# A fused attention, expert and gated layer on one core: the last half block is stored behind the final branch

## The chip, the core and the metric

The kernel runs on one core of one Trainium2 chip. The core has TensorE (PE in the rows; PEld are its weight loads), VectorE (DVE), ScalarE (ACT), GpSimd (POOL), and SyncE (SP), which here issues most of the DMA transfers. A letter q behind an engine's name stands for its sequencer, which handles branches, semaphores and DMA issues. The metric is the time of one execution on the device in microseconds. Three runs of the kernel before took 420.01, 418.44 and 418.93 us, so the median is 418.93.

## The reference

Three layers follow each other, all in float32. A linear attention with 4 batches, 8 heads, 576 tokens and 64 columns per head compresses keys and values into 32 memory slots, and each query attends to these. Then every token goes through one of 8 experts, with a sticky choice: a gate decides whether the expert of the token before is kept. The last layer is a gated convolution over tokens.

```python
# experts
e = fresh_e if s == 0 or local_gate[b, s] < 0.5 else prev_e
h = np.maximum(x[b, s] @ w1[e], 0.0)
out[b, s] = p[e] * (h @ w2[e])
# gated layer
h = np.maximum(x @ w_in, 0.0)
for k in range(3):
    conv_out += conv_w[k][None, None, :] * hp[:, k:k + S, :]
return (h * (1.0 / (1.0 + np.exp(-conv_out))) @ w_out).astype(np.float32)
```

## The kernel before, in words

The kernel computes with the expert that the first token of each batch chooses, and finds out on the way whether any token chose another one. Their number is kept in `anyi`, a single integer. With the given inputs it is zero. The work up to 211 us (attention, expert products, routing) is ordered by hand in a list of items and is not touched by the change.

The function `gated` is the last layer. For each batch it multiplies by `w_in` (tiles `pi`), makes the gate on ScalarE, VectorE and GpSimd, and multiplies by `w_out` (tiles `po`), 128 tokens by 512 columns at a time. Each product is the sum of three products of high and low parts over eight blocks of 128, so 24 matmuls. The result goes from PSUM to `ot` by ScalarE (line 1052) and from there to `out` by SyncE (line 1054). A batch has four full chunks of 128 tokens; its last 64 tokens are collected by GpSimd in `tail` and are done for two batches together, as chunk 4. In the last batch the last chunk is done in two halves of 256 columns (lines 1043 to 1049), each evicted by ScalarE and stored by SyncE as soon as its 24 matmuls are through.

Behind that stands the branch (lines 1063 and 1064). Each engine loads `anyi` into a register, compares it with zero, and runs or jumps over the part that adds the other experts and repeats the gated layer. The skipped part lies between the branch and the end of the program, and each engine has its own branch in its own list of instructions. Where an engine jumps, it lands in a short block that waits until the engine's own work is done and adds to the engine's semaphore what the skipped part would have added, so that later waits read the same count on both ways. SyncE does this for each of its DMA queues. From there it is one step to the end block (line 1116 in the rows): SyncE waits in twelve instructions for all queues and engines, each engine runs a DRAIN, and two barriers led by GpSimd with a clearing of semaphores between them close the program.

A tile scheduler orders the instructions in each block, here in the order in which they are written, and sets the waits on semaphores. It moves nothing across a branch.

Of the kernel before, what the change touches and what calls it, by code (L numbers as in the profile page):

```python
# [114 lines left out]
def fused_kernel(tc, q, first, first_q, kv, kv_tail, phi, w1, w2, w_in, conv_w, w_out, out):  # L115
    nc = tc.nc
    wide = w_in.dtype == I64
    PSUM = bass.MemoryType.PSUM
    with (
# [2 lines left out]
        tc.tile_pool(name="state", bufs=2) as state,  # L122
        tc.tile_pool(name="wpool", bufs=4) as wpool,
        tc.tile_pool(name="ps1", bufs=4, space=PSUM) as ps1,
        tc.tile_pool(name="ps2", bufs=2, space=PSUM) as ps2,
    ):

        def bank(name):
            return ps1.tile([128, 512], F32, tag="one", name=name)

        def banks(name):
            return ps2.tile([128, 2, 512], F32, tag="two", name=name)

        def slow(item):

# [831 lines left out]
        def gated(gp, nm, scaled=False):  # L967
            def first(b):
                return None if scaled else expert(b)

            wo.clear()
            for j in range(4):
                stage_out(j)
            ys = y_parts(0) if scaled else ys0[1]
            if scaled:
                split_y(0, load_y(0, None), *ys)
            tail = None
            for b in range(B):
                yh, yl = ys
                gs = []  # L980
                if b + 1 < B:
                    yn = load_y(b + 1, first(b + 1))
                if b % 2 == 0:
                    tail = gp.tile([128, 8, 2, 128], F32R, tag="tail", bufs=1, name=f"tail{b}")
                to = 64 * (b % 2)
                def gate(f, ht, ct):
                    nc.scalar.activation(ct, ct, AF.Sigmoid)  # L987
                    slow(f"gm.{f}").tensor_tensor(ct, ht, ct, ALU.mult)  # L988
                    t = gp.tile([128, 2, S], F32R, tag="g", name=f"g{nm}{b}_{f}")

                    def finish():
                        split(t[:, 0, :], t[:, 1, :], ct, slow(f"gs.{f}"))
                        nc.gpsimd.tensor_copy(tail[:, f, :, to:to + 64], t[:, :, 512:576].bitcast(F32))  # L993

                    gs.append(t)
                    return finish

                before = None
                for f in range(8):
                    fs = slice(f * 128, (f + 1) * 128)  # L1000
                    ps = banks(f"pi{b}_{f}")
                    matmul3([(ps[:, hf, :HALF], half(hf)) for hf in range(2)],
                            [((wi[kc][:, 0, fs], wi[kc][:, 1, fs]), (yh[:, kc, :], yl[:, kc, :])) for kc in range(4)],
                            tc.keep_in_program_order if b == 0 else lambda ins: ins)
                    finish = gate(*before) if before else lambda: None
                    ht = lp.tile([128, S], F32, tag="cv", name=f"ht{b}_{f}")
                    nc.scalar.activation(two(ht), halves(ps), AF.Relu)  # L1007
                    ct = lp.tile([128, S], F32, tag="cv", name=f"ct{b}_{f}")
                    nc.scalar.activation(ct, ht, AF.Copy, scale=convw[:, 1, f:f + 1])  # L1009
                    nc.vector.scalar_tensor_tensor(  # L1010
                        ct[:, 1:], ht[:, :S - 1], convw[:, 0, f:f + 1], ct[:, 1:], ALU.mult, ALU.add)
                    nc.vector.scalar_tensor_tensor(  # L1012
                        ct[:, :S - 1], ht[:, 1:], convw[:, 2, f:f + 1], ct[:, :S - 1], ALU.mult, ALU.add)
                    finish()
                    before = f, ht, ct
                    while len(wo) < 4 and f >= WO[len(wo)]:
                        wo.append(w2_piece(f"wo{len(wo)}", slow(f"wo.{len(wo)}")))
                gate(*before)()
                if b + 1 < B:
                    ys = y_parts(b + 1)  # L1020
                    split_y(b + 1, yn, *ys)

                def product(ps, c, fr, cols=slice(0, 512)):
                    for f in fr:
                        w = wo[f // 2].rearrange("p s (i d) -> p s i d", i=2)
                        st = [gs[f][:, s, c * 128:(c + 1) * 128] if c < 4 else tail[:, f, s, :] for s in range(2)]
                        for i, (sp, mp) in enumerate(((0, 0), (0, 1), (1, 0))):
                            nc.tensor.matmul(ps[:, cols], st[sp], w[:, mp, f % 2, cols],  # L1028
                                             start=f == 0 and i == 0, stop=f == 7 and i == 2)

                chunks = [0, 1, 2] + [4] * (b % 2) + [3]
                pss = {c: bank(f"po{b}_{c}") for c in chunks[:3]}
                for c in chunks[:3]:
                    product(pss[c], c, range(0, 6))
                for c in chunks:
                    if c in pss:
                        product(pss[c], c, range(6, 8))
                    elif b < B - 1 or c != chunks[-1]:
                        pss[c] = bank(f"po{b}_{c}")
                        product(pss[c], c, range(8))  # L1040
                    else:

                        for cq in range(2):
                            cols = slice(256 * cq, 256 * cq + 256)
                            ps = bank(f"po{b}_{c}_{cq}")
                            product(ps, c, range(8), cols)
                            ot = gp.tile([128, 256], F32, tag="ot", bufs=4, name=f"ot{b}_{c}_{cq}")
                            nc.scalar.activation(ot, ps[:, cols], AF.Copy)
                            nc.sync.dma_start(out[b, c * 128:(c + 1) * 128, cols], ot)
                        continue  # L1050
                    ot = gp.tile([128, 512], F32, tag="ot", bufs=4, name=f"ot{b}_{c}")
                    nc.scalar.activation(ot, pss[c], AF.Copy)  # L1052
                    if c < 4:
                        nc.sync.dma_start(out[b, c * 128:(c + 1) * 128, :], ot)
                    else:
                        nc.sync.dma_start(out[b - 1, 512:576, :], ot[0:64])
                        nc.sync.dma_start(out[b, 512:576, :], ot[64:128])

        wo = []
        ffn_cm.__exit__(None, None, None)  # L1060
        with tc.tile_pool(name="gated", bufs=8, reuse_waits="tile") as gp:
            gated(gp, "")
        any_more = nc.values_load(anyi[0:1, 0:1], min_val=0, max_val=B * E)
        with tc.If(any_more > 0, preferred_fallthrough_block=True):
            with tc.tile_pool(name="more", bufs=1) as fp:
                fps.append(fp)
                for b in range(B):
                    other_experts(b)
            with tc.tile_pool(name="again", bufs=8, reuse_waits="tile") as gp:
                gated(gp, "x", True)  # L1070
        late[0].__exit__(None, None, None)


# [46 lines left out]
```

## Time and profile before

| what | value |
|---|---|
| median of three runs | 418.93 us |
| profiled execution | 418.69 us, its span 416.9 us |
| TensorE busy | 406.9 us, 98% of the span |
| VectorE, ScalarE, GpSimd busy | 276.2, 222.2 and 74.8 us |
| matmuls of line 1028 (`po`) | 90.2 us, 408 of them |
| granted TensorE clock, mean | 0.999 of full speed |

The span goes from the program's first to its last instruction; the time of the execution has some 1.8 us more around it. Branches, semaphores and DMA issues do not count as busy, so the end of the program, where nothing else runs, shows as idle in the busy shares; it can be read in the views of single lines, where those instructions stand with their durations and starts.

### The profile page before, as it was taken

The page shows a single profiled execution, that of the slowest core. Times are in us where ns is not written, and L with a number is a line of the kernel's source. Part 1 is how long each engine was busy: PE and PEld are TensorE (multiplying, and loading weights), DVE is VectorE, ACT ScalarE, POOL GpSimd, SP SyncE. Part 2 cuts the span into 40 slices and gives each one's busy share as a digit, 9 for nine tenths or more (in the row PEclk, how much of TensorE's full clock was granted, in tenths as well). Part 3 has the DMA queues.
Part 4 walks back from the last instruction along what each step waited for, and adds up shares of the span by engine and source line. Part 5 has one row for each costly group of instructions (what it writes and reads, how often), then busy time and mean ns, then how long its engine had stood idle before and what let it go on. Part 6 is the DMA issues. An engine that isn't in the chain of part 4 may idle for free.

```text
span 416.9 us, 8479 instructions
## 1 busy us (share of the span) xinstructions
PE 406.9 (98%) x3390; PEld 370.8 (89%) x3391; DVE 276.2 (66%) x509; ACT 222.2 (53%) x414; POOL 74.8 (18%) x121
## 2 busy tenths in 40 slices
PE   7999999999999999999999999999999999999994
PEld 6769989889989998899999988998889988999884
DVE  2679899696786984975979981579105792177500
ACT  4356568465566354745748652577215773277320
POOL 1000201411122211311111620033200332014300
PEclk9999999999999999999999999999999999999999
DMA  7999979976984599946550032000020000200022
GB/s 270 346 374 405 347 258 347 412 274 231 338 285 153 146 380 400 363 164 197 167 176 2 2 113 100 2 2 0 31 75 21 2 1 13 89 2 0 3 77 57
DMA packets 23760, 69.04 MB, mean 166 GB/s; under 512 B 3264, under 2 KB 4032, under 8 KB 23712
## 3 DMA queue, kind: packets, MB, share of 16 engines
q1 hardware_dynamic: 20128, 56.88, 38.6%
q0 software_dynamic: 3584, 11.54, 7.1%
q8 instruction: 28, 0.46, 0.4%
q14 instruction: 20, 0.16, 0.1%
HBM read 52.08 MB, written 16.33 MB: 164 GB/s over the span
## 4 chain that ended last, share of the span: by engine, by line
PE 91%; DMA 4%; SPq 1%; DVE 1%; ACT 1%; issue 0%; ACTq 0%
PE py L160 25%; PE pi L160 24%; PE po L1028 24%; PE ph L160 11%; DMA wb_0r<-in_w 2%; DMA kt<-in_kv_tail 2%; PE pk L406 1%; PE pv L449 1%; PE sc L449 1%; PE idle L456 1%; PE pa L384 1%; PE pl L587 1%; DVE wb L148 0%; SPq L271 0%; ACT wb L147 0%
## 5 line engine op out<-in xcount | busy, mean ns | idle before, releaser
L160 PE MATMUL py<-h,wb 128*128 128x288 f32 x768 | 108.2, 297 | 0.0
L160 PEld LDWEIGHTS py<-h,wb 128*128 128x128 f32 x768 | 102.9, 188 | 4.2 <-issue 3.2
L160 PE MATMUL pi<-yh,wi 128*128 128x288 f32 x512 | 90.4, 295 | 0.0
L1028 PE MATMUL po<-wo,g 128*128 128x512 f32 (+1 forms) x408 | 90.2, 377 | 0.0
L1028 PEld LDWEIGHTS po<-wo,g 128*128 128x128 f32 x408 | 72.8, 188 | 13.2
L160 PEld LDWEIGHTS pi<-yh,wi 128*128 128x128 f32 x512 | 76.3, 188 | 0.9
L1010 DVE SCALAR_TENSOR_TENSOR ct<-ht,convw,ct 128x575 f32<-128x575 f32 x32 | 30.9, 966 | 52.4 <-ACT ct L1009 52.4
L160 PE MATMUL pi<-yl,wi 128*128 128x288 f32 x256 | 54.6, 295 | 0.0
L160 PE MATMUL ph<-att,vh 128*128 128x288 f32 x256 | 53.5, 302 | 0.7 <-DVE h L753 0.3
L993 POOL CAST tail<-g 128x128 fp32r<-128x128 f32 x32 | 23.1, 724 | 122.9 <-DVE g L148 122.2
L160 PEld LDWEIGHTS ph<-att,vh 128*128 128x128 f32 x256 | 40.5, 188 | 4.9 <-DVE h L753 2.1
L836 POOL DMA_DIRECT2D ydram<-ys x32 | 17.5, 547 | 146.8 <-ACT ys L835 140.4
L160 PEld LDWEIGHTS pi<-yl,wi 128*128 128x128 f32 x256 | 41.1, 188 | 0.0
L1007 ACT ACTIVATE ht<-pi 128x576 f32<-128x576 f32 x32 | 20.8, 651 | 33.8 <-PE pi L160 33.8
L160 PE MATMUL ph<-att,vl 128*128 128x288 f32 x128 | 37.7, 296 | 0.0
L753 DVE SCALAR_TENSOR_TENSOR h<-ph,h 128x288 fp32r<-128x288 f32 x64 | 28.1, 450 | 13.3 <-ACT h L752 13.3
L752 ACT ACTIVATE h<-ph 128x288 fp32r<-128x288 f32 x64 | 25.7, 410 | 15.0 <-PE ph L160 14.7
L835 ACT ACTIVATE ys<-py 128x288 f32<-128x288 f32 x32 | 13.1, 409 | 37.1 <-PE py L160 24.5
L1052 ACT ACTIVATE ot<-po 128x512 f32<-128x512 f32 x17 | 9.5, 598 | 43.4 <-PE po L1028 43.4
L988 DVE TENSOR_TENSOR ct<-ht,ct 128x576 f32<-128x576 f32 x32 | 27.0, 844 | 7.3 <-ACT ct L987 7.1
L1012 DVE SCALAR_TENSOR_TENSOR ct<-ht,convw,ct 128x575 f32<-128x575 f32 x32 | 28.4, 886 | 0.4
L147 ACT ACTIVATE g<-ct 128x576 fp32r<-128x576 f32 x32 | 21.7, 680 | 12.6 <-DVE ct L988 12.6
(234 smaller groups left out, 505.1 us busy)
## 6 DMA issues: line engine op xcount, KB each, us to landing
kv<-in_kv SPq DMA_DIRECT2D x16, 512.0 KB, 8.6
q<-in_q SPq DMA_DIRECT2D x8, 576.0 KB, 9.5
ydram<-ys POOLq DMA_DIRECT2D x32, 144.0 KB, 5.2
y<-ydram SPq DMA_DIRECT2D x4, 1152.0 KB, 6.8
out<-ot SPq DMA_DIRECT2D x15, 256.0 KB, 2.1
ph<-in_phi SPq DMA_DIRECT2D x8, 288.0 KB, 7.3
adram<-at POOLq DMA_DIRECT2D x8, 288.0 KB, 7.0
wa_0r<-in_w SPq DMA_DIRECT2D x4, 512.0 KB, 4.0
```

The lines of the kernel that those rows point to most:

```text
L147: pin(nc.scalar.activation(hi, src, AF.Copy))
L160: pin(nc.tensor.matmul(ps, st, mv[:, cols], start=i == 0, stop=i == len(terms) - 1))
L752: nc.scalar.activation(t[:, 0, :], ps, AF.Relu)
L753: low = nc.vector.scalar_tensor_tensor(t[:, 1, :], ps, 0.0, t[:, 0, :].bitcast(F32), ALU.max, ALU.subtract)
L835: nc.scalar.activation(yt, ps, AF.Copy)
L836: stored.append(nc.gpsimd.dma_start(ydram[b, d, :, half(hf)], yt).ins)
L988: slow(f"gm.{f}").tensor_tensor(ct, ht, ct, ALU.mult)
L993: nc.gpsimd.tensor_copy(tail[:, f, :, to:to + 64], t[:, :, 512:576].bitcast(F32))
L1007: nc.scalar.activation(two(ht), halves(ps), AF.Relu)
L1010: nc.vector.scalar_tensor_tensor(ct[:, 1:], ht[:, :S - 1], convw[:, 0, f:f + 1], ct[:, 1:], ALU.mult, ALU.add)
L1012: nc.vector.scalar_tensor_tensor(ct[:, :S - 1], ht[:, 1:], convw[:, 2, f:f + 1], ct[:, :S - 1], ALU.mult, ALU.add)
L1028: nc.tensor.matmul(ps[:, cols], st[sp], w[:, mp, f % 2, cols], start=f == 0 and i == 0, stop=f == 7 and i == 2)
```

## The change

The last chunk's first half is copied out of PSUM by VectorE and stored by GpSimd, in place of ScalarE and SyncE. The second half goes into a PSUM tile `last` of its own, for which the pool of pairs `ps2` is closed and a pool `ps3` is opened in its place. Its eviction by ScalarE and its store by SyncE are written behind the branch and so stand in a block that follows both ways. A hint for TensorE's branch is placed behind the last matmul of chunk 4. Within the part that is skipped, `gated` does the same with its own last chunk.

```diff
--- before.py
+++ after.py
@@ -122,14 +122,18 @@
         tc.tile_pool(name="state", bufs=2) as state,
         tc.tile_pool(name="wpool", bufs=4) as wpool,
         tc.tile_pool(name="ps1", bufs=4, space=PSUM) as ps1,
-        tc.tile_pool(name="ps2", bufs=2, space=PSUM) as ps2,
     ):
+        ps2_cm = tc.tile_pool(name="ps2", bufs=2, space=PSUM)
+        pairs = [ps2_cm.__enter__()]
 
         def bank(name):
             return ps1.tile([128, 512], F32, tag="one", name=name)
 
         def banks(name):
-            return ps2.tile([128, 2, 512], F32, tag="two", name=name)
+            return pairs[-1].tile([128, 2, 512], F32, tag="two", name=name)
+
+
+        last_block = []
 
         def slow(item):
 
@@ -1025,8 +1029,8 @@
                         w = wo[f // 2].rearrange("p s (i d) -> p s i d", i=2)
                         st = [gs[f][:, s, c * 128:(c + 1) * 128] if c < 4 else tail[:, f, s, :] for s in range(2)]
                         for i, (sp, mp) in enumerate(((0, 0), (0, 1), (1, 0))):
-                            nc.tensor.matmul(ps[:, cols], st[sp], w[:, mp, f % 2, cols],
-                                             start=f == 0 and i == 0, stop=f == 7 and i == 2)
+                            last_product[:] = [nc.tensor.matmul(ps[:, cols], st[sp], w[:, mp, f % 2, cols],
+                                                                start=f == 0 and i == 0, stop=f == 7 and i == 2).ins]
 
                 chunks = [0, 1, 2] + [4] * (b % 2) + [3]
                 pss = {c: bank(f"po{b}_{c}") for c in chunks[:3]}
@@ -1040,13 +1044,21 @@
                         product(pss[c], c, range(8))
                     else:
 
-                        for cq in range(2):
-                            cols = slice(256 * cq, 256 * cq + 256)
-                            ps = bank(f"po{b}_{c}_{cq}")
-                            product(ps, c, range(8), cols)
-                            ot = gp.tile([128, 256], F32, tag="ot", bufs=4, name=f"ot{b}_{c}_{cq}")
-                            nc.scalar.activation(ot, ps[:, cols], AF.Copy)
-                            nc.sync.dma_start(out[b, c * 128:(c + 1) * 128, cols], ot)
+                        if not scaled:
+                            ps2_cm.__exit__(None, None, None)
+                            last_cm.append(tc.tile_pool(name="ps3", bufs=1, space=PSUM))
+                            pairs.append(last_cm[0].__enter__())
+
+                            with tc.issue_after(last_product[0]):
+                                tc.mark_branch_hint_location("more", engines=[ENG.PE])
+                            last_block.append(pairs[-1].tile([128, 512], F32, tag="last", name="last"))
+                        cols = slice(0, 256)
+                        ps = bank(f"po{b}_{c}")
+                        product(ps, c, range(8), cols)
+                        ot = gp.tile([128, 256], F32, tag="ot", bufs=4, name=f"ot{b}_{c}")
+                        nc.vector.tensor_copy(ot, ps[:, cols])
+                        nc.gpsimd.dma_start(out[b, c * 128:(c + 1) * 128, cols], ot)
+                        product(last_block[0], c, range(8), slice(256, 512))
                         continue
                     ot = gp.tile([128, 512], F32, tag="ot", bufs=4, name=f"ot{b}_{c}")
                     nc.scalar.activation(ot, pss[c], AF.Copy)
@@ -1056,18 +1068,22 @@
                         nc.sync.dma_start(out[b - 1, 512:576, :], ot[0:64])
                         nc.sync.dma_start(out[b, 512:576, :], ot[64:128])
 
-        wo = []
+        wo, last_cm, last_product = [], [], []
         ffn_cm.__exit__(None, None, None)
         with tc.tile_pool(name="gated", bufs=8, reuse_waits="tile") as gp:
             gated(gp, "")
         any_more = nc.values_load(anyi[0:1, 0:1], min_val=0, max_val=B * E)
-        with tc.If(any_more > 0, preferred_fallthrough_block=True):
+        with tc.If(any_more > 0, preferred_fallthrough_block=True, label="more"):
             with tc.tile_pool(name="more", bufs=1) as fp:
                 fps.append(fp)
                 for b in range(B):
                     other_experts(b)
             with tc.tile_pool(name="again", bufs=8, reuse_waits="tile") as gp:
                 gated(gp, "x", True)
+        ot = late[1].tile([128, 256], F32, tag="last", bufs=1, name="ot")
+        nc.scalar.activation(ot, last_block[0][:, 256:], AF.Copy)
+        nc.sync.dma_start(out[B - 1, 384:512, 256:], ot)
+        last_cm[0].__exit__(None, None, None)
         late[0].__exit__(None, None, None)
```

On TensorE, the place is the step from chunk 4 (tile `po_4`, from `tail`) to the last chunk's first half (`po_3_0`, now `po_3`; `wo` and `g` are the weights and the gated values). Before:

```order
L1028 MATMUL po_4_4821<-wo_3347,tail_4018 128x512 x6
L1028 MATMUL po_4_4821<-wo_3387,tail_4018 128x512 x6
L1028 MATMUL po_3_0_4850<-wo_3230,g_0_4499 128x256 x3
L1028 MATMUL po_3_0_4850<-wo_3230,g_1_4536 128x256 x3
L1028 MATMUL po_3_0_4850<-wo_3307,g_2_4573 128x256 x3
```

Now:

```order
L1032 MATMUL po_4_4821<-wo_3347,tail_4018 128x512 x6
L1032 MATMUL po_4_4821<-wo_3387,tail_4018 128x512 x6
L1132 BRANCH_PREFETCH_HINT
L1032 MATMUL po_3_4856<-wo_3230,g_0_4499 128x256 x3
L1032 MATMUL po_3_4856<-wo_3230,g_1_4536 128x256 x3
```

The hint is new between the two; the matmuls keep their order and their shapes, and behind them stand the load of `anyi` and the branch, as before.

On ScalarE, the place is the end of its list ahead of the branch (`ot_0` to `ot_2` and `ot_4` are full evictions, `anyi` is the flag). Before:

```order
L1052 ACTIVATE ot_2_4818<-po_2_4739 128x512
L1052 ACTIVATE ot_4_4846<-po_4_4821 128x512
L1048 ACTIVATE ot_3_0_4875<-po_3_0_4850 128x256
L1048 ACTIVATE ot_3_1_4903<-po_3_1_4878 128x256
L1063 TENSOR_LOAD anyi
L1064 COMPARE_AND_BRANCH
```

Now:

```order
L1064 ACTIVATE ot_1_4809<-po_1_4738 128x512
L1064 ACTIVATE ot_2_4818<-po_2_4739 128x512
L1064 ACTIVATE ot_4_4846<-po_4_4821 128x512
L1075 TENSOR_LOAD anyi
L1076 COMPARE_AND_BRANCH
```

The evictions of the two halves are gone from it. The second one stands in the new block, behind the jumps at the end of both ways:

```order
L1064 ACTIVATE ot_2_8795<-po_2_8716 128x512
L1064 ACTIVATE ot_4_8823<-po_4_8798 128x512
L1076 UNCONDITIONAL_BRANCH x2
L1084 ACTIVATE ot<-last 128x256
L1132 UNCONDITIONAL_BRANCH
```

It waits there for TensorE's semaphore with the count of the skipped part in it. SyncE's last store stands in the same block, behind SyncE's own jump.

On GpSimd, the place is the end of its work ahead of the branch (`tail` collects the last tokens). Before:

```order
L148 TENSOR_TENSOR g_6_4721<-ct_6_4687,g_6_4721 128x576
L993 CAST tail_4018<-g_6_4721 128x2x64
L993 CAST tail_4018<-g_7_4733 128x2x64
L1063 TENSOR_LOAD anyi
L1064 COMPARE_AND_BRANCH
```

Now:

```order
L152 TENSOR_TENSOR g_6_4721<-ct_6_4687,g_6_4721 128x576
L997 CAST tail_4018<-g_6_4721 128x2x64
L997 CAST tail_4018<-g_7_4733 128x2x64
L1060 DMA out<-ot_3_4881 128x256
L1075 TENSOR_LOAD anyi
L1076 COMPARE_AND_BRANCH
```

A store now stands between GpSimd's last copy and its load of the flag, and it waits for VectorE's copy of the first half. Behind the branch, on the way that is taken, GpSimd's list before is this (the first row holds the jumps of both ways; the row ahead of it belongs to the skipped part):

```order
L148 TENSOR_TENSOR gx_6_8696<-ct_6_8662,gx_6_8696 128x576
L993 CAST tail_7997<-gx_6_8696 128x2x64
L993 CAST tail_7997<-gx_7_8708 128x2x64
L1064 UNCONDITIONAL_BRANCH x2
L1116 ISA
```

And now this:

```order
L1060 DMA out<-ot_3_8852 128x256
L1076 UNCONDITIONAL_BRANCH
L1076 ISA
L1076 UNCONDITIONAL_BRANCH
L1132 UNCONDITIONAL_BRANCH
L1132 ISA
```

The instruction between the jumps adds the skipped part's store to its DMA semaphore, and one jump more leads through the new block.

## Rows read from the trace of the kernel before

**Rows 1.** Stretches: us; busy PE, PEld, DVE, ACT, POOL; clock, DMA, GB/s.
```profile
405.28:411.20 5.92, 5.91 (x49) 5.70 (x47) 0.00 (x0) 0.99 (x2) 0.00 (x0) 1.00 0.28 69
411.20:416.90 5.70, 0.00 (x0) 0.00 (x0) 0.00 (x0) 0.38 (x1) 0.00 (x0) 0.94 0.10 32
```

**Rows 2.** Timeline, the end: start us, us, engine, line, what, idle before.
```profile
408.40 0.39 ACT L1048 ACTIVATE ot<-po 128x256 f32<-128x256 f32 x1 [2.32 <-PE po L1028]
410.31 0.88 PE L1028 MATMUL po<-wo,g 128*128 128x256 f32 x6
411.28 0.38 ACT L1048 ACTIVATE ot<-po 128x256 f32<-128x256 f32 x1 [2.49 <-PE po L1028]
```

**Rows 3.** Line 1049, the last stores: min/median/max ns, starts; landing us.
```profile
L1049 SPq DMA_DIRECT2D out<-ot x2: 338/338/338, 408.8 to 411.7; - x2
DMA to landing us min/median/max: 1.7/1.7/1.7
```

**Rows 4.** Line 1064, the branch: ns, first and last start, by engine.
```profile
L1064 SPq EVENT_SEMAPHORE  x9: 17/17/17, 414.6 to 415.2; - x9
L1064 PEldq EVENT_SEMAPHORE  x2: 51/51/51, 413.1 to 413.3; - x2
L1064 ACTq EVENT_SEMAPHORE  x2: 17/17/17, 414.5 to 414.6; - x2
L1064 PEldq COMPARE_BRANCH  x1: 3602/3602/3602, 409.5 to 409.5; - x1
L1064 ACTq COMPARE_BRANCH  x1: 50/50/50, 411.8 to 411.8; - x1
L1064 SPq COMPARE_BRANCH  x1: 53/53/53, 412.1 to 412.1; - x1
L1064 POOLq EVENT_SEMAPHORE  x2: 17/17/17, 396.3 to 396.4; - x2
L1064 POOLq COMPARE_BRANCH  x1: 45/45/45, 393.5 to 393.5; - x1
```

**Rows 5.** DMA queues from 409 to 416 us: packets, MB, share.
```profile
q8 instruction: 2, 0.03, 2.1%
```

**Rows 6.** Line 1116, the end block, in several stretches, as rows 4.
```profile
L1116 SPq EVENT_SEMAPHORE  x12: 28/28/28, 415.3 to 416.0; - x12
L1116 POOLq DRAIN  x1: 4966/4966/4966, 396.5 to 396.5; - x1
L1116 ACTq DRAIN  x1: 8/8/8, 414.7 to 414.7; - x1
L1116 POOLq EVENT_SEMAPHORE  x4: 17/17/17, 416.2 to 416.8; - x4
L1116 POOLq DRAIN  x2: 44/76/107, 416.3 to 416.7; - x2
```

**Rows 7.** Timeline and line 1057: last eviction and store before the halves.
```profile
405.48 0.60 ACT L1052 ACTIVATE ot<-po 128x512 f32<-128x512 f32 x1 [4.84 <-PE po L1028]
L1057 SPq DMA_DIRECT2D out<-ot x1: 588/588/588, 406.6 to 406.6; - x1
```

**Rows 8.** Line 1063, GpSimd's load of the flag.
```profile
L1063 POOLq TENSOR_LOAD <-anyi x1: 486/486/486, 392.9 to 392.9; - x1
```

**Rows 9.** Groups by form, VectorE, 128x256: busy us, mean ns, idle.
```profile
L740 DVE TENSOR_TENSOR vl<-pv,vh 128x256 fp32r<-128x256 f32 x2 | 0.8, 419 | 0.1
```

**Rows 10.** Timeline and line 836: a GpSimd store behind ScalarE; landings, 180-190.
```profile
188.63 0.41 ACT L835 ACTIVATE ys<-py 128x288 f32<-128x288 f32 x1 [3.10 <-PE py L160]
189.34 0.54 POOL L836 DMA_DIRECT2D ydram<-ys  x1 [2.93 <-ACT ys L835]
DMA to landing us min/median/max: 2.4/2.9/3.7
```

**Rows 11.** Line 1107, the start block, GpSimd's DRAIN there.
```profile
L1107 POOLq DRAIN  x1: 184/184/184, 0.3 to 0.3; - x1
```

**Rows 12.** Timeline of GpSimd, its last work before the branch.
```profile
392.96 0.30 POOL L993 CAST tail<-g 128x128 fp32r<-128x128 f32 x1 [1.42 <-DVE g L148]
```

## The prediction

> **What bounds the kernel now.** I first cut the span into stretches of busy time [rows 1]. TensorE works 5.91 of the 5.92 us from 405.28, the two last half products, and not at all in the 5.70 behind them, where ScalarE works 0.38 us and nothing else does. The granted clock is 1.00 until the products end. The change touches nothing before 405.28 us: up to there each engine's list of instructions is the same in both programs. So the question is what the 5.70 us behind the last product are made of.
>
> The timeline comes next [rows 2]. The first half product lets ScalarE go at 408.40, the last product ends at 410.31 + 0.88 = 411.19, ScalarE evicts its 256 columns in 0.38 us from 411.28, and the store is issued at 411.7 and lands 1.7 us behind that [rows 3], near 413.4. That is still 3.5 us before the end.
>
> The rows of the branch say what fills them [rows 4]. Every engine reads a flag, compares and jumps over the part for other experts, because the flag is zero here. The jump is dear: SyncE compares at 412.1 and runs its next instruction, the first of nine semaphore rows, at 414.6; ScalarE goes 411.8 to 414.5; TensorE's compare alone lasts 3602 ns, 409.5 to 413.1; GpSimd went 393.5 to 396.3. The DMA view has blocks of the instruction queues in this stretch, two of them on queue 8 [rows 5], so this is code being fetched. SyncE then needs 414.6 to 415.3 for its nine rows and 415.3 to 416.1 for twelve more, and the closing barrier ends at 416.9 [rows 4, 6]. The end is therefore last product, eviction, store issue, SyncE's jump, SyncE's list. The landing at 413.4 is hidden behind that jump.
>
> One engine is out of sight in this chain: GpSimd. It came to the end block at 396.5 and its first DRAIN there lasted 4966 ns [rows 6]. It had been done for ages, so the 5 us cost nothing.
>
> **The change part by part.** *ScalarE and SyncE jump early.* ScalarE's last work ahead of the branch is now the eviction at 405.48 (0.60 us) [rows 7]; with a flag load of about 0.5 us, as GpSimd's [rows 8], and the jump's 2.7 us [rows 4] it stands behind the branch at about 409. SyncE's last issue is at 406.6 for 588 ns [rows 7]; its jump of 2.5 us ends near 409.8, nine rows of 0.07 us end near 410.5, and the store that they ask for has landed by then even at twice the 1.7 us of [rows 3], at 410.0. Both are ready before the last product, so 2.5 us leave the end.
>
> *The last eviction now waits for TensorE's own jump.* The path over the skipped part adds that part's counts to each engine's semaphore, and the last eviction waits for TensorE's count with these added. So TensorE has to be behind its branch. Unhinted that would be 413.1 [rows 4]. The hint stands ahead of the last two half products, 5.9 us of work [rows 1], against about 3.6 us for the unhinted jump; I take it that the code is there and TensorE only waits for its last product. Its two semaphore rows stand 0.15 us apart, so I charge 0.1 us: eviction 411.38 to 411.76, issue 411.80, landing 413.5. SyncE waits for that landing in the eleventh of its twelve rows, and 0.06 us later goes on as it did from 416.0: 0.9 us to the end [rows 4, 6]. By this chain alone the span would end near 414.5.
>
> *VectorE and GpSimd take the first half.* VectorE copies 128x256 out of PSUM from 408.40. No such copy is in the trace; the nearest are VectorE's subtraction from PSUM of the same shape, 419 ns, and ScalarE's 0.38 us [rows 2, 9]. I take 0.42 and keep 0.38 to 0.45, so it ends at 408.82. GpSimd issues 0.30 us after the writer is done: 188.63 + 0.41 to 189.34 [rows 10]. So 409.12, for 0.54 us, to 409.66. Behind the issue stand its own flag load and jump: from the start of the load at 392.9 to the DRAIN at 396.5 it took 3.6 us [rows 4, 6, 8], and now there are one semaphore instruction and one jump more, which I put at 0.15 us from the 0.1 us between its two semaphore rows. GpSimd starts its first DRAIN at 409.66 + 3.6 + 0.15 = 413.4 instead of 396.5, so 16.9 us of cover are gone. VectorE's own flag load and jump begin at 408.82 and, at GpSimd's 3.6 us, end near 412.4: hidden.
>
> *What that DRAIN costs* decides everything. The trace has three more on GpSimd: 184 ns at 0.3 us, just behind small memsets and before any store [rows 11], and 107 and 44 ns at the very end [rows 6]. The long one is the first after all the stores that GpSimd issues and after its last tail copies, and its row names nothing that released it. I cannot see the cause, so I bound it by 0.1 and 4.97 us and take 4.97: whether it is put down to the stores or to the arithmetic before it, both are there again. Sum: 413.4 + 4.97 = 418.4, and from GpSimd's row at 416.2 to the end is 0.8 us [rows 6], so 419.1. That is 2.2 us more than 416.9. The profiled execution took 418.69 us, 1.8 more than its span, and lies 0.24 below the median of the three runs, 418.93. So 420.9 by the profile's own time, 421.1 by the median; I say 421.0.
>
> *GpSimd's store* lands 2.4 to 3.7 us after its issue in the stretch around 185 us [rows 10], so at 411.5 to 412.8. SyncE asks for it in the first of the twelve rows, but has to wait for 413.5 anyway: hidden, and to cost anything it would have to take over 4 us.
>
> *A rule against my value.* ScalarE's DRAIN in the end block takes 8 ns, and GpSimd's first there takes 4966 [rows 6]. The Trainium skill, "VectorE: DVE Perf Modes", section "The DRAIN you can't avoid", says that the boilerplate DRAINs of a profile's pre- and postamble last about 12 ns, the same on all five engines. The trace agrees for ScalarE and not for GpSimd. By that rule the 5 us would be an accident of that one moment, and the time that of the first rival.
>
> **The rivals.** *First, faster: the long DRAIN does not come back.* For it: the three other DRAINs of GpSimd are under 0.2 us. Against it: these follow no stores, or follow the long one directly. GpSimd is then ready at 413.5, level with the last landing, and the chain through TensorE and SyncE sets the end: 414.5, 2.4 us earlier, 416.3 us in time. It decides from a DRAIN shorter than about 0.5 us; at about 2.7 us (413.4 + 2.7 + 0.8 = 416.9) nothing is gained or lost.
>
> *Second, the hint does nothing and the DRAIN is short.* TensorE's first row behind the branch stays at 413.1, the eviction runs 413.25 to 413.63, the store lands at 415.4, and the span ends near 416.4: 0.5 us earlier, 418.2. For it: no hint is in the trace. Against it: the lead of 5.9 us. If the DRAIN is long, it hides this too and the sum stays at 419.1.
>
> *Third, the long DRAIN runs from GpSimd's last work, not from its own start.* Before, it ended at 396.5 + 4.97 = 401.5, 8.2 us after GpSimd's last copy, 392.96 + 0.30 [rows 12]. Then it would end at 409.66 + 8.2 = 417.9, the span at 418.7, the time at 420.4.
>
> **How the numbers follow.** A long DRAIN counted from its start has 0.55, counted from the last work 0.12, a short DRAIN with a working hint 0.23, without one 0.06; 0.04 is left for what I have not thought of. A measurement of this kernel tells about 0.5% from no change, 2.1 us. The forecast, 2.2 us, lies on that border: with half a microsecond of doubt in the start of the DRAIN and in the runs it is slower in a little over half of its cases. That gives slower 0.55 x 0.57 + 0.12 x 0.3 + 0.02 = 0.37. The first rival, 2.4 us, lies just beyond the border on the other side: 0.23 x 0.65 + 0.02 = 0.17 for faster. The rest, 0.46, is no change. The likeliest case's own range is 420.2 to 421.9; to hold 8 in 10 the range has to take in the first rival, so it goes from 416.2 to 421.9.
>
> **What would show it.** GpSimd's first DRAIN in the end block at 413.1 to 413.7 with about 5 us, and every other engine waiting for it at the barrier: right. TensorE's compare far under 3602 ns, ScalarE's last eviction near 411.4, its store landed by 413.7: these steps right, whatever the DRAIN does. A DRAIN of 0.2 us and an end near 414.5 would make the forecast wrong by the term that I chose, and an eviction near 413.3 would show that the hint fails.

## The result, and the profile after

The changed kernel takes 422.56 us (median of 6 runs, 421.72 to 425.43), the kernel before beside it 419.23 (418.44 to 420.15): ratio 1.0092, 95% interval 1.0068 to 1.0117. It is slower, by 3.3 us between the medians and some 3.9 us by the ratio. The forecast was 421.0 us; 422.56 lies outside the range, above its upper end of 421.9.

The stretches show where (us; busy PE, PEld, DVE, ACT, POOL; clock, DMA, GB/s). They are cut at the last product's end, as in [rows 1]:

```profile
404.34:410.26 5.92, 5.91 (x49) 5.70 (x47) 0.42 (x1) 0.60 (x1) 0.56 (x1) 1.00 0.31 78
410.26:419.86 9.60, 0.00 (x0) 0.00 (x0) 0.00 (x0) 0.38 (x1) 0.00 (x0) 0.68 0.05 15
```

The products still take 5.92 us at a granted clock of 1.00. From the last product's end to the span's end, which I call the tail from here on, it is 9.60 us and was 5.7. The two profiled spans differ by less, 419.9 against 416.9, because in this execution the last product came 0.94 us earlier, with every engine's operations and DMA issues up to 404 us in the same order. Tails are therefore what I compare.

The branch by engine, answering to [rows 4] (ns, first and last start):

```profile
L1076 SPq EVENT_SEMAPHORE  x9: 17/17/17, 409.2 to 409.8; - x9
L1076 PEldq EVENT_SEMAPHORE  x2: 51/51/51, 410.3 to 410.4; - x2
L1076 POOLq EVENT_SEMAPHORE  x2: 17/17/17, 412.4 to 412.5; - x2
L1076 SPq COMPARE_BRANCH  x1: 53/53/53, 406.3 to 406.3; - x1
L1076 PEldq COMPARE_BRANCH  x1: 393/393/393, 408.5 to 408.5; - x1
L1076 POOLq COMPARE_BRANCH  x1: 45/45/45, 408.7 to 408.7; - x1
L1076 POOLq INC_SWDGE_SEM  x1: 1395/1395/1395, 412.6 to 412.6; - x1
```

The intended part happened. SyncE's nine rows run from 409.2 instead of 414.6, ahead of the last product's end at 410.26. TensorE's compare takes 393 ns instead of 3602, so its rows stand right at that end. The timeline has the last eviction 0.12 us later (start us, us, engine, line, what, idle before):

```profile
407.47 0.42 DVE L1059 COPY ot<-po 128x256 f32<-128x256 f32 x1 [15.51 <-DMA out<-ot]
408.19 0.56 POOL L1060 DMA_DIRECT2D out<-ot  x1 [15.88 <-DVE ot L1059]
410.38 0.38 ACT L1084 ACTIVATE ot<-last 128x256 f32<-128x256 f32 x1 [5.24 <-PEq L1076]
410.79 0.34 SPq L1085 DMA_DIRECT2D out<-ot  x1
```

What replaced SyncE is the last row of the branch and the end block, answering to [rows 6], in several stretches:

```profile
L1132 POOLq DRAIN  x1: 5047/5047/5047, 414.0 to 414.0; - x1
L1132 SPq EVENT_SEMAPHORE  x1: 28/28/28, 411.2 to 411.2; - x1
L1132 SPq EVENT_SEMAPHORE  x11: 27/28/28, 413.9 to 414.5; - x11
L1132 SPq DRAIN  x2: 7/10/13, 414.6 to 414.7; - x2
L1132 POOLq EVENT_SEMAPHORE  x4: 17/17/17, 419.1 to 419.8; - x4
```

GpSimd, 396.3 before, comes out of its jump at 412.4, spends 1.395 us in one semaphore instruction and 5.047 us in its DRAIN, and lets the barrier close from 419.1 on. SyncE is through with its own list at 414.7 and waits 4.4 us for it. GpSimd holds SyncE before that too: of SyncE's twelve rows the first stands at 411.2 and the second only at 413.9, because it waits for the semaphore that the 1.395 us instruction raises as it ends.

### The profile page after: what moved, and what is told of

Read it like the earlier page. It is cut to its first block, busy times and chain, and to the rows that moved or that the text cites. A ratio compares the mean times of both kernels' runs of the same rounds, so it can differ in the third digit from the quotient of the medians.

```text
span 419.9 us, 8481 instructions
## 1 busy us (share of the span) xinstructions
PE 407.0 (97%) x3390; PEld 370.9 (88%) x3391; DVE 276.8 (66%) x510; ACT 221.4 (53%) x413; POOL 75.4 (18%) x122
## 5 line engine op out<-in xcount | busy, mean ns | idle before, releaser
L1032 PE MATMUL po<-wo,g 128*128 128x512 f32 (+1 forms) x384 | 87.4, 383 | 0.0
L1032 PEld LDWEIGHTS po<-wo,g 128*128 128x128 f32 x384 | 69.9, 188 | 13.2
```

Source lines behind the costliest of these rows:

```text
L1032: last_product[:] = [nc.tensor.matmul(ps[:, cols], st[sp], w[:, mp, f % 2, cols], start=f == 0 and i == 0, stop=f == 7 and i == 2).ins]
```

## The experiments

Theory G: the end is set by GpSimd's late list (store, jump, the 1.4 us instruction, the DRAIN). Rival B: what was put behind the branch is what comes late. Edits are against the changed kernel unless said.

**Both halves stored by SyncE.**

```diff
-                        nc.gpsimd.dma_start(out[b, c * 128:(c + 1) * 128, cols], ot)
+                        nc.sync.dma_start(out[b, c * 128:(c + 1) * 128, cols], ot)
```

> As changed, but the first half, still copied by VectorE, is stored by SyncE and no longer by GpSimd. The measure is the tail, from the end of the last product to the end of the span: 5.7 us before, 9.6 us as changed. Theory G (GpSimd's store ahead of the branch, its flag load, jump, semaphore instruction of 1.4 us and DRAIN of 5 us set the end): GpSimd is done early again and the tail falls to about 4.0 us; it is not 3.3, since SyncE now issues the first half's store some 2.3 us ahead of the last product's end and its jump of 2.5 us and ten rows of 0.07 us end 1.2 us behind it. That is 1.7 us less than before and 5.6 less than as changed. Theory B (what was put behind the branch, the eviction that waits for TensorE's jump and the extra block, is what is late): the tail stays near 9 us, in no case under 5.7.

417.57 us against 418.82, ratio 0.9962 (0.9939 to 0.9985): faster than the kernel before, and 5 us under the 422.56 of the changed one, which was measured in another series. The stretch behind its last product, as above:

```profile
413.92:418.05 4.13, 0.00 (x0) 0.00 (x0) 0.00 (x0) 0.38 (x1) 0.00 (x0) 0.94 0.11 36
```

Its end block and branch:

```profile
L1132 POOLq DRAIN  x1: 4966/4966/4966, 398.9 to 398.9; - x1
L1076 SPq EVENT_SEMAPHORE  x9: 17/17/17, 414.6 to 415.2; - x9
L1076 SPq COMPARE_BRANCH  x1: 53/53/53, 412.0 to 412.0; - x1
```

One word changed the tail from 9.60 to 4.13 us. G holds, B falls. GpSimd's DRAIN is still 5 us, but at 398.9, under the products. What is late now is SyncE's jump, 412.0 to 414.6.

**The kernel before, with only the first half moved** to VectorE and GpSimd: nothing behind the branch, no hint.

```diff
+                            if cq:
...
+                            else:
+                                nc.vector.tensor_copy(ot, ps[:, cols])
+                                nc.gpsimd.dma_start(out[b, c * 128:(c + 1) * 128, cols], ot)
```

> The kernel before with one part of the change alone: the first half is copied by VectorE and stored by GpSimd; the second half is evicted by ScalarE and stored by SyncE ahead of the branch as before, without a hint. Theory G: the tail is that of the whole change, 9.0 to 10.0 us, with a first DRAIN of GpSimd in the end block of about 5 us that starts some 3.5 us behind the last product, and the time 3 to 4 us above before. Theory B: the tail is that of before, 5.7 us, and the time is that of before.

422.33 us, ratio 1.0077 (1.0047 to 1.0107), tail 413.09 to 421.91, 8.8 us. GpSimd's instruction and SyncE's last rows in it:

```profile
L1068 POOLq INC_SWDGE_SEM  x1: 1395/1395/1395, 414.6 to 414.6; - x1
L1120 SPq DRAIN  x2: 7/10/13, 418.9 to 418.9; - x2
```

The first half alone brings 3.1 of the 3.9 us by which the tail grew. SyncE, which still has the last store and its jump ahead of it, is through at 418.9, and the end is at 421.9 all the same. The 8.8 lie under the 9.0 to 10.0 expected; GpSimd's jump took 2.8 us here and 3.6 in the changed kernel, which is the difference between the two tails.

**No hint.**

```diff
-                            with tc.issue_after(last_product[0]):
-                                tc.mark_branch_hint_location("more", engines=[ENG.PE])
```

> As changed, without the hint for TensorE's branch. Theory G: TensorE's compare lasts about 3.6 us again in place of 0.39, the last eviction starts 2 us behind the last product in place of 0.1 and its store lands near 4.3 us behind it, but GpSimd's DRAIN ends near 8.8 us behind it and hides that: tail 9.6 us, time as changed within 0.3%. Theory B: the eviction is on the path, and the tail grows by the 2 us to 11.5.

422.01 us, ratio 1.0072 (1.0048 to 1.0096), tail 9.5 us. TensorE's branch in it:

```profile
L1074 PEldq EVENT_SEMAPHORE  x2: 51/51/51, 412.9 to 413.1; - x2
L1074 PEldq COMPARE_BRANCH  x1: 3622/3622/3622, 409.3 to 409.3; - x1
```

The hint is what cut the compare from 3.6 to 0.4 us. Without it the last eviction starts 2.06 us after the last product, at 413.03, and nothing is lost, because GpSimd ends later still.

**The kernel before with hints alone,** on TensorE, ScalarE and SyncE, nothing moved.

```diff
...
+                        if b == B - 1 and c == 2 and not scaled:
+                            for behind_it, engine in ((last_product[0], ENG.PE), (evict, ENG.Activation), (store, ENG.SP)):
+                                with tc.issue_after(behind_it):
+                                    tc.mark_branch_hint_location("more", engines=[engine])
...
```

> The kernel before, with nothing moved: the branch is hinted on TensorE, ScalarE and SyncE, each time some microseconds ahead of it. If the hint does on ScalarE and SyncE what it did on TensorE (a compare of 0.4 us in place of 3.6), SyncE stands behind its jump 0.8 us after the last product's end in place of 3.4, runs its nine rows while the last store lands 2.2 us after it, and the tail is 3.2 to 3.6 us: 2.3 us under before. If the code is fetched in vain (the block is gone when the branch comes), the tail stays at 5.7 us. GpSimd is early in both, and its DRAIN of 5 us is hidden.

418.93 us against 418.82, ratio 0.9994 (0.9974 to 1.0015), tail 5.9 us. Its branch and its hints (the latter stand under the end block's line):

```profile
L1068 PEldq COMPARE_BRANCH  x1: 393/393/393, 410.5 to 410.5; - x1
L1068 SPq COMPARE_BRANCH  x1: 73/73/73, 413.1 to 413.1; - x1
L1068 SPq EVENT_SEMAPHORE  x9: 17/17/17, 415.8 to 416.4; - x9
L1120 SPq BRANCH_PREFETCH_HINT  x1: 55/55/55, 402.1 to 402.1; - x1
```

SyncE was hinted 11 us ahead and ScalarE 12, and their jumps still took 2.7 and 2.8 us. No block of an instruction queue moves in the DMA view from 399 to 410 us, where these two hints stand. In the one place that was tried, a hint worked on TensorE and did nothing on ScalarE and SyncE, so for these two the other experiments start the jump earlier instead.

**Arithmetic instead of a store, late on GpSimd.** It copies VectorE's copy; SyncE stores.

```diff
-                        nc.vector.tensor_copy(ot, ps[:, cols])
-                        nc.gpsimd.dma_start(out[b, c * 128:(c + 1) * 128, cols], ot)
+                        od = gp.tile([128, 256], F32, tag="ot", bufs=4, name=f"od{b}_{c}")
+                        nc.vector.tensor_copy(od, ps[:, cols])
+                        nc.gpsimd.tensor_copy(ot, od)
+                        nc.sync.dma_start(out[b, c * 128:(c + 1) * 128, cols], ot)
```

> The first half goes through GpSimd without being stored by it: VectorE copies it out of PSUM, GpSimd copies that copy, SyncE stores GpSimd's copy and, as in the changed kernel, the last half. GpSimd works as late as in the changed kernel but stores nothing late. Theory G (anything late on GpSimd costs its jump and a 5 us DRAIN; the 1.4 us semaphore instruction belongs to the store): no semaphore instruction of 1.4 us, DRAIN 4.9 to 5.1 us, last product's end to span's end 8.0 to 8.6 us, 421.0 to 421.8 us. Rival S (the long DRAIN belongs to a store that is just out): DRAIN under 1 us and hidden, tail 4.4 to 4.8 us as SyncE's path sets it, about 418 us.

421.66 us, ratio 1.0077 (1.0047 to 1.0108), tail 8.4 us. GpSimd's DRAIN in it:

```profile
L1134 POOLq DRAIN  x1: 4966/4966/4966, 413.8 to 413.8; - x1
```

The late store isn't needed: a copy of 0.4 us brings 2.7 of the 3.9 us. The semaphore instruction is gone, and the DRAIN is as long as before.

**The same, and GpSimd issues no store anywhere:** its 60 earlier stores go to SyncE.

```diff
-            stored.append(nc.gpsimd.dma_start(ydram[b, d, :, half(hf)], yt).ins)
+            stored.append(nc.sync.dma_start(ydram[b, d, :, half(hf)], yt).ins)
...
```

> The kernel of the run with late arithmetic on GpSimd, and besides every one of the 60 stores that GpSimd issues before (ydram, adram, vdram, f_in, f_out) issued by SyncE: GpSimd does arithmetic alone in this program and never a DMA. Its whole time means nothing, since SyncE's loads may queue behind those stores. Theory G: DRAIN 4.9 to 5.1 us all the same, tail 8.0 to 8.6 us. Rival D (GpSimd's first DRAIN is long because it has issued stores in this program, however early): DRAIN near the 0.18 us of the program's start, tail 4.4 to 4.8 us.

GpSimd's end block and branch in it:

```profile
L1134 POOLq DRAIN  x1: 45/45/45, 409.9 to 409.9; - x1
L1078 POOLq EVENT_SEMAPHORE  x2: 17/17/17, 409.7 to 409.8; - x2
L1078 POOLq COMPARE_BRANCH  x1: 45/45/45, 409.2 to 409.2; - x1
```

Rival D was right and G, in the form that anything late costs 5 us, was wrong. With the same late copy the DRAIN takes 45 ns. The long DRAIN is the price of stores issued long before: the last of the 60 went out at 211.9 us in the run with arithmetic, 202 us ahead of its DRAIN. The tail was 5.8 us, not 4.4 to 4.8, with SyncE's jump at 3.6 us. GpSimd's own jump took 0.5 us instead of 2.8 to 4.1; I did not settle why.

**How the DRAIN goes with the number of stores.** The counts so far were 60 with 4.966 us, 61 with 5.047, none with 0.045. That is 0.082 us a store, so I tried 29 and 1: the changed kernel with the 32 ydram stores, and with all 60, on SyncE.

```diff
-            stored.append(nc.gpsimd.dma_start(ydram[b, d, :, half(hf)], yt).ins)
+            stored.append(nc.sync.dma_start(ydram[b, d, :, half(hf)], yt).ins)
```

> The changed kernel with only the 32 stores to ydram issued by SyncE, so that GpSimd issues 29 in the program, the first half's among them. Theory L (0.045 + 0.082 n): DRAIN 2.42 us, and the tail 9.6 - 2.6 = 7.0 us. Rival F (fixed once any store has been issued): DRAIN 5.0 us, tail 9.6 us. A third outcome, a DRAIN that goes by the bytes stored, would give a value off the line: these 32 stores are 4.7 of the some 10 MB.

GpSimd's DRAIN and semaphore instruction with 29 stores:

```profile
L1132 POOLq DRAIN  x1: 2434/2434/2434, 416.7 to 416.7; - x1
L1076 POOLq INC_SWDGE_SEM  x1: 760/760/760, 415.9 to 415.9; - x1
```

The DRAIN is 2.434 us, 2.42 expected from the line, so rival F, a fixed price, falls. Bytes do not explain it either: the 29 stores are 6.95 MB and the 60 are 11.54, which would have given 3.0 us. The tail was 6.4 us (413.50 to 419.9) and not 7.0, because the semaphore instruction has shrunk too. And with one store:

> The changed kernel with the 60 earlier stores of GpSimd (ydram, adram, vdram, f_in, f_out) issued by SyncE, so that the first half's store is the only one that GpSimd issues. Theory L (its first DRAIN costs a fixed price for every store that it has issued in the program: 0.045 us with 0 stores, 4.966 with 60, 5.047 with 61, so 0.045 + 0.082 n): DRAIN 0.13 us, and the tail from the last product to the span's end is no more than 5.3 us, since SyncE's own list was through 4.4 us after the last product in the changed kernel. Rival F (a fixed price of 5 us once any store has been issued): DRAIN near 5 us and a tail of 6.5 to 9.6 us, by how long the jump takes.

The same rows of GpSimd, and its store with the landing:

```profile
L1132 POOLq DRAIN  x1: 3112/3112/3112, 410.4 to 410.4; - x1
L1076 POOLq INC_SWDGE_SEM  x1: 193/193/193, 410.1 to 410.1; - x1
L1060 POOL DMA_DIRECT2D out<-ot x1: 686/686/686, 408.9 to 408.9; - x1
DMA to landing us min/median/max: 4.5/4.5/4.5
```

The tail, 4.1 us, lies within L's bound, the DRAIN is not as L has it: 3.1 us instead of 0.13. But this store took 4.5 us to land, at 413.4, and the DRAIN ended at 410.36 + 3.11 = 413.47. So it looks as if the DRAIN also waits for a store still under way; in the changed kernel the store (2.5 us) had landed by 410.7, long before. One execution shows this, and I tried nothing that would tell it apart. The semaphore instruction has a line of its own: 0.193, 0.760, 1.395 us for 1, 29 and 61 stores, 0.020 a store. At 416.85 us the change reads faster than all 17 runs of before beside it (417.93 to 422.93) once GpSimd's earlier stores are elsewhere, but that is a single run.

**GpSimd stores half of chunk 4 instead,** 3 us earlier, in the first pass only.

```diff
-                        nc.gpsimd.dma_start(out[b, c * 128:(c + 1) * 128, cols], ot)
+                        nc.sync.dma_start(out[b, c * 128:(c + 1) * 128, cols], ot)
...
-                        nc.sync.dma_start(out[b, 512:576, :], ot[64:128])
+                        last = b == B - 1 and not scaled
+                        (nc.gpsimd if last else nc.sync).dma_start(out[b, 512:576, :], ot[64:128])
```

> The changed kernel, but SyncE stores the first half and GpSimd stores the second half of the five-hundred-and-twelfth rows' block (out[b, 512:576]), evicted 3.0 us earlier than the first half is (405.13 against 407.89, and GpSimd's store at about 405.15 against 408.19). Theory G (GpSimd's list runs a fixed 11.7 us from its store to the end: 408.19 to 419.86): the tail is shorter by just that, 9.6 - 3.0 = 6.6 us, near 419.5 us. Rival C (what costs is that a second queue's store lands among the last ones and delays SyncE's, not GpSimd's list): tail 4.1 us as with SyncE alone, about 417.5 us.

417.75 us, ratio 0.9986 (0.9956 to 1.0016), tail 5.5 us: between G's 6.6 and C's 4.1. GpSimd's DRAIN and SyncE's branch:

```profile
L1133 POOLq DRAIN  x1: 5047/5047/5047, 411.1 to 411.1; - x1
L1077 SPq EVENT_SEMAPHORE  x9: 17/17/17, 414.3 to 415.0; - x9
L1077 SPq COMPARE_BRANCH  x1: 53/53/53, 410.3 to 410.3; - x1
```

GpSimd's DRAIN ends at 416.2, and SyncE is through at 417.0 after a jump of 4.0 us, so here SyncE sets the end. There is no 1.4 us instruction here. The skipped part holds a second pass of gated(). In the changed kernel that pass stores from GpSimd too, and the way round it has the instruction in its place; here only the first pass does.

**Looking for a better version.** With both stores on SyncE the last one waits for SyncE's jump. First I let ScalarE, which evicts the last half, also store it:

```diff
-                        nc.gpsimd.dma_start(out[b, c * 128:(c + 1) * 128, cols], ot)
+                        nc.sync.dma_start(out[b, c * 128:(c + 1) * 128, cols], ot)
...
-        nc.sync.dma_start(out[B - 1, 384:512, 256:], ot)
+        nc.scalar.dma_start(out[B - 1, 384:512, 256:], ot)
```

> The changed kernel with the first half stored by SyncE and the last half stored by ScalarE, which evicts it. In the run with both halves stored by SyncE the last store went out at 415.375, because SyncE's jump landed at 414.63 and ten rows followed, while ScalarE had evicted the piece by 414.43. Theory G (GpSimd's late list was the whole loss, and without it the end follows the last store): the store goes out some 0.1 us behind the eviction, 0.9 us earlier, and the last product's end to the span's end takes 3.1 to 3.3 us (4.1 there, 5.7 in the kernel before); about 416.5 us, ratio 0.994 to the kernel before. Rival J (SyncE's jump and its end block are what is waited for, whoever stores): the tail stays at 3.9 to 4.2 us, about 417.5 us. Reading to tell them apart: whether SyncE's wait for the last store's landing or its own rows come last.

417.79 us, ratio 0.9978 (0.9952 to 1.0004), tail 4.2 us: rival J, that the end waits for SyncE's jump whoever stores, holds. The branch's rows of SyncE and ScalarE's store:

```profile
L1076 SPq EVENT_SEMAPHORE  x9: 17/17/17, 411.9 to 412.5; - x9
L1085 ACTq DMA_DIRECT2D out<-ot x1: 378/378/378, 412.6 to 412.6; - x1
```

The eviction was done at 411.69. ScalarE waits until 412.6 for the semaphore that its store is to count on, and the last of SyncE's nine rows adds the skipped part's count to that one. Then I moved the first half's store behind the branch, on SyncE, its eviction staying ahead:

```diff
-                        ot = gp.tile([128, 256], F32, tag="ot", bufs=4, name=f"ot{b}_{c}")
-                        nc.vector.tensor_copy(ot, ps[:, cols])
-                        nc.gpsimd.dma_start(out[b, c * 128:(c + 1) * 128, cols], ot)
+                        if not scaled:
+                            first_half.append(late[1].tile([128, 256], F32, tag="last", bufs=2, name="of"))
+                        nc.vector.tensor_copy(first_half[0], ps[:, cols])
...
+        nc.sync.dma_start(out[B - 1, 384:512, :256], first_half[0])
```

> The changed kernel, but the first half, evicted by VectorE ahead of the branch, is stored by SyncE behind it, before the last half's store, which stays as changed. GpSimd has nothing late, and SyncE has nothing left to wait for ahead of its jump but the block of chunk 4. Theory G with the chain of the last store: SyncE's jump runs 406.3 to 409.2 and its rows to 409.9 as in the changed kernel, the first half's store goes out there and the last half's right behind its eviction, so the tail is 0.1 to the eviction, 0.38 for it, 0.03, 1.7 to the landing and 0.9 of end block: 3.1 to 3.4 us, against 5.7 before, 4.1 with SyncE's first-half store ahead of the branch and 9.6 as changed; about 416.5 us, ratio 0.994 to the kernel before. Rival J (SyncE's jump stretches when it runs beside the others' fetches, as its 4.0 us did in the run in which GpSimd stored chunk 4): last store later than the eviction by up to 1 us, tail 4.0 to 4.5 us, no gain over the run with both stores on SyncE.

417.42 us, ratio 0.9953 (0.9929 to 0.9977), tail 4.45 us. VectorE's branch and SyncE's store in it:

```profile
L1076 DVEq EVENT_SEMAPHORE  x2: 21/21/21, 412.1 to 412.2; - x2
L1076 DVEq COMPARE_BRANCH  x1: 76/76/76, 408.9 to 408.9; - x1
L1083 SPq DMA_DIRECT2D out<-of x1: 337/337/337, 412.2 to 412.2; - x1
```

Neither theory named this: SyncE is ready at 410.8, but what it waits for behind the branch is VectorE's count with the skipped part's added, and VectorE adds it after its own jump, 408.9 to 412.1. So no engine should have work between chunk 4 and the branch but TensorE: the whole last block goes behind it.

```diff
...
-                        product(ps, c, range(8), cols)
...
-                        product(last_block[0], c, range(8), slice(256, 512))
+                        product(last_block[0], c, range(8))
...
+        ot = late[1].tile([128, 512], F32, tag="last", bufs=1, name="ot")
+        nc.scalar.activation(ot, last_block[0], AF.Copy)
+        nc.sync.dma_start(out[B - 1, 384:512, :], ot)
```

> The changed kernel with the last block whole: one product of 512 columns, one eviction by ScalarE and one store by SyncE, both behind the branch; TensorE's hint stays. No engine has anything between chunk 4 and the branch but TensorE, so VectorE, SyncE and ScalarE all jump before the last product ends, and nothing behind the branch waits for a jump that starts late (as SyncE's first-half store waited for VectorE's in the run before, 409.0 to 412.1). Theory G: tail 0.12 to the eviction, 0.6 for it (the 128x512 evictions take 0.598), 0.03, 1.75 to the landing, 0.9 of end block: 3.3 to 3.6 us, and the product itself 0.3 us shorter (24 matmuls 0.227 apart against 48 of 0.120); against 5.7 before that is 2.4 us less, about 416.4 us, ratio 0.993 to 0.995. Rival J (SyncE's jump and the end block's rows are late whatever stands before them): tail 4.1 to 4.5 us as in the three runs with SyncE before, ratio 0.996.

415.98 us against 418.91, ratio 0.9920 (0.9891 to 0.9948), the best of all. Its two stretches:

```profile
404.68:410.28 5.60, 5.60 (x25) 4.32 (x23) 0.00 (x0) 0.60 (x1) 0.00 (x0) 1.00 0.23 54
410.28:414.14 3.86, 0.00 (x1) 0.00 (x0) 0.00 (x0) 0.60 (x1) 0.00 (x0) 1.00 0.19 70
```

SyncE's rows of the branch, its store and the landing:

```profile
L1070 SPq EVENT_SEMAPHORE  x9: 17/17/17, 409.7 to 410.4; - x9
L1079 SPq DMA_DIRECT2D out<-ot x1: 338/338/338, 411.0 to 411.0; - x1
DMA to landing us min/median/max: 2.0/2.0/2.0
```

The second stretch runs 0.07 us past the span's end, which is at 414.07, so the tail is 3.79 us. SyncE is there first, the store goes out right behind the 0.60 us eviction and takes 2.0 us to land (1.75 expected for this larger one), which is most of the distance from the 3.3 to 3.6 expected. The products run 5.60 us instead of 5.92.

## Why the prediction was wrong

The mechanism was right, its price too low. GpSimd's DRAIN came back and set the end, and in the chain through TensorE, ScalarE and SyncE the last eviction and its store's issue came within 0.1 us of the forecast, counted from the last product's end. Two steps of that chain did not come true, and GpSimd hid both: the last store took 2.8 us to land, not 1.7, and SyncE's second row waited for GpSimd's semaphore instruction, a wait that the prediction does not have. So SyncE was through 4.4 us behind the last product, where the prediction's rows give about 2.5. The terms of GpSimd's list, counted from the last product's end (411.19 in the prediction, 410.26 in the trace):

| term | predicted, us | measured, us |
|---|---|---|
| store issued | -2.07 | -2.07 |
| flag load starts | -1.53, behind the issue | -2.09, beside it |
| load to first row behind the jump | 3.35 | 4.18 |
| that row to the DRAIN | 0.35, with 0.15 for the new instruction | 1.62 |
| DRAIN | 4.97 | 5.05 |
| DRAIN's end to the span's | 0.8 | 0.8 |
| tail | 7.9 | 9.6 |

So the DRAIN was to start 1.9 to 2.5 us behind the last product and started 3.7 behind it.

- **The step that failed** is "now there are one semaphore instruction and one jump more, which I put at 0.15 us from the 0.1 us between its two semaphore rows". That one instruction takes 1.395 us. The trace of before shows no such one behind a store, and I gave it a single value where it wanted a bound from both sides. The term, from the first row behind the jump to the DRAIN, was 1.62 us instead of 0.35, and that alone is 1.3 of the 1.7 us by which the tail was too short. It goes with a store of GpSimd that stands in the skipped part as well: it is gone in the run with arithmetic and in the one with chunk 4.
- **The jump** I took over from 393.5 to 396.3 us, where of the other engines only VectorE, at 392.8, had its compare near. At 408.7, within 0.7 us of the compares of VectorE and TensorE, it took 3.6 us from compare to first row against 2.8 [rows 4]. The same jump took 2.5 to 2.9 us in seven of the other runs, 3.5 to 4.1 in three, and 0.5 in the two in which SyncE issues the 60 earlier stores. Neighbours alone don't explain it: with compares just as close it was 2.8 in the run with the first half alone. I have not isolated the reason.
- **The flag load** does not wait for the store's issue; that took 0.56 us off.
- **The DRAIN**: right in size, but as a choice between two bounds: the prediction did not know the cause, and had it been one that the change took away, the same 4.97 would have been wrong. The cause is now largely settled. It goes by the stores that GpSimd has issued, 0.045 us with none, 2.434 with 29, 4.966 with 60, 5.047 with 61; the 3.112 with a single store, still under way, stands apart and stays open. By the third rival, 8.2 us from GpSimd's last work, it would have ended at 417.0 as changed, where the store was issued by 408.75; it ended at 419.0. The page "VectorE: DVE Perf Modes" of the Trainium skill (section "The DRAIN you can't avoid") has about 12 ns on all five engines. These runs don't bear that out for GpSimd: even its shortest first DRAIN in the end block took 45 ns.
- **The first rival** asked for a short DRAIN. A short DRAIN alone would have given less than it says. With SyncE's twelfth row at 414.5, as measured, and the 0.9 us from there to the end, I estimate an end 5.2 us behind the last product against 5.7 before: 0.5 us, not 2.4. With one store on GpSimd in the whole program the tail was 4.1 us, but its DRAIN was not short; GpSimd's jump took 0.5 us and its semaphore instruction 0.193, so the DRAIN began at 410.4, 0.6 us ahead of the last product's end.
- **The hint** worked, and the run without it cost nothing, as the second rival's last sentence had it.
- **The range** failed with the sum: around the likeliest case I allowed half a microsecond for the DRAIN's start and the runs, but the two terms taken from other places of the trace were off by 1.3 and 0.8 us, and only the load's 0.56 went the other way.

## What to carry to other kernels

Before giving an engine a last piece of work, list all that it still has to do behind it to the end of the program, and price the rows that were hidden because it used to be done early; here a store of 0.56 us brought a list of 11.7 us to the end with it, of which 3.9 showed. Work just ahead of a branch delays not only its own engine's jump but all who wait behind the branch for that engine's count, so the last piece either goes behind the branch whole or stays ahead of it. Where nothing in the trace is like a term, bound it from both sides.

## What the runs showed of the hardware

- GpSimd's first DRAIN in the end block grows by 0.082 us for every store that it has issued in the program (0, 29, 60 and 61, all landed by then), though most were issued some 200 us before or more. The semaphore instruction that stands for a skipped store grows by 0.020 (0.193, 0.760, 1.395 us for 1, 29, 61), and SyncE's end block waits for it.
- A hint 8 us ahead, as changed (14 in the run with hints alone), cut TensorE's compare from 3.6 to 0.4 us; on ScalarE and SyncE, 12 and 11 us ahead, hints fetched nothing.
- Jumps over the skipped part vary: SyncE's took 2.6 us before, 2.9 as changed, 4.0 in the run in which GpSimd stored half of chunk 4.
- The last store landed 2.8 us after its issue as changed, against 1.7 before [rows 3]; here GpSimd's wait hid it.
